# One kernel under an order of its own: a list scheduler, lanes in pairs, four shared PSUM tiles

## The chip, the cores and the metric

The kernel runs on one core of a Trainium2 chip. The metric is device time in microseconds (us). TensorE is called PE here, VectorE DVE, ScalarE ACT, GpSimd POOL and SyncE SP; PEld is PE's weight load.

## The reference, cut to what matters

All tensors are bf16, with S = 2048 positions, D = 640 channels and F = 1728. With x = q:

- `kv = shift(k) * v`, where shift is a causal convolution with 4 taps for each channel.
- `y = causal_conv(kv, ssm_k) + kv * ssm_D`: a convolution of length 2048 for each channel (an FFT of 4096 in the reference).
- `h = x + layernorm(x) * y`
- `out = h + (silu(z @ w_gate) * (z @ w_up)) @ w_down`, with `z = layernorm(h)`.

## The kernel before, in words

**Tiling.** The 2048 positions are cut into four blocks of 512 (`NB` = 4), and block i needs the blocks before it through the long convolution. The convolution is done in a transformed domain: `x_transform` (L289 to L317) multiplies kv by constant cosine and sine tables on PE (L300), evacuates on ACT (L133) and combines on DVE into six lanes, S, D and E for two parities. `g_load`, `g_fold` and `g_transform` (L218 to L268) do the same to the four pieces of the filter. `half_sum` (L213) makes each S lane of the filter.

**A block's convolution.** For block i the six accumulators are the sum over j of X[j] * H[i-j], lane by lane on DVE: products at L514, L522, L534 and L537, sums at L526 and L538. The lanes of filter pieces 1 to 3 and of blocks 0 and 1 go to DRAM on POOL's queue (`store_lane`, L206) and come back on SP's (`load_lane`, L210). `back` (L357 to L397) combines the accumulators on DVE, transforms them back on PE (L379), evacuates (L381), forms h, takes the layernorm's sums on ACT (`ln_stats`, L335 and L336; for block 0 partly on DVE, L332), the power on POOL (L346), and transposes the normalised h on PE (L395) into `hlnT`.

**A block's FFN.** `ffn` (L399 to L450): 27 passes of five gate or up matmuls (L428) into four one-bank PSUM tiles, Silu (L432) and copy (L433) on ACT, their product `tT` on DVE (L434); then 4 row tiles of 28 down matmuls (L444), evacuation (L447), the addition of h on DVE (L449), and the store on POOL's queue (L450).

**Order.** The tile framework's planner orders the instructions by priorities (`at`): block i's convolution has U*(i+1), its FFN U*(i+2.5), the rest of the filter (PREP) comes behind block 0's convolution. Every engine then carries out its own list in that order. PSUM is two two-bank tiles (`psM`) for all but gate and up, and four one-bank tiles (`psF`) for these. `hlnT` and `tT` have one buffer each, so the gate and up of block i+1 wait for the transposes of block i+1 and for the down matmuls of block i. At the start block 0's k is loaded in pieces (`load_k`, L154): the rows of partitions 16 to 127 on SP's queue, the rest in five small DMAs on ACT's queue, among ACT's own work.

Of the kernel before, what the change touches and what calls it, by code (L numbers as in the profile page):

```python
# [28 lines left out]
NSP, NWK, NWG = 20, 7, 3  # L29
LANES = [(l, e) for l in ("S", "D", "E") for e in range(2)]  # L30
# [6 lines left out]
def make_consts():  # L37

# [18 lines left out]
    po = -so[:, None] * np.sin(np.outer(to, m))  # L57
# [9 lines left out]
    return bf(cs), bf(gb), bf(ci)  # L67


@with_exitstack  # L70
def kernel(
# [45 lines left out]
    def spt(name):  # L117
        return sp.tile([P, 2, D], BF16, name=name, tag="sp", bufs=NSP)

    def h0t(name):  # L120
        return sp.tile([P, 2, D], BF16, name=name, bufs=1)

    def wkt(name, shape=(P, NS, D)):
        return wk.tile(list(shape), BF16, name=name, tag="wk", bufs=NWK)

    def ps_mm():
        return psM.tile([P, 2, 512], FP32, name="ps_mm")

    def evac(dst, ps, dve=False):
        if dve:  # L130
            nc.vector.tensor_copy(v2(dst), r3(ps))
        else:
            nc.scalar.copy(v2(dst), r3(ps))  # L133
# [19 lines left out]

    def load_k(i):  # L154
        kt = wk.tile([P, NS + 3, D], BF16, name="krun", bufs=1)
        if i == 0:
            nc.vector.memset(kt[0:1, 0:3, :], 0.0)
            nc.scalar.dma_start(out=kt[0:1, 3:7, :], in_=kk[0:NS, :].rearrange("(o r) d -> o r d", o=1))
            lo = P
            while lo > 1:  # L160

                hi, lo = lo, 16 if lo == P else lo // 2
                (nc.sync if hi == P else nc.scalar).dma_start(
                    out=flat(kt[lo:hi, :, :]),
                    in_=bass.AP(tensor=kk.tensor, offset=kk.offset + (NS * lo - 3) * D, ap=[[NS * D, hi - lo], [1, 7 * D]]))
        else:
            nc.sync.dma_start(out=flat(kt[:]), in_=rows(kk, i, -3, 7))
        return kt

    def load4(t, i, name):  # L170
        x = wkt(name)
        nc.sync.dma_start(out=flat(x[:]), in_=rows(t, i))
        return x

    cs_t = cpool.tile([P, NS, 2, HALF], BF16, name="cs_t")
    gb_t = cpool.tile([P, 2, 4, HALF], BF16, name="gb_t")
    ci_t = cpool.tile([P, 2, 2, NS, P], BF16, name="ci_t")
    wd_t = cpool.tile([P, 14, D], BF16, name="wd_t")
    w4 = cpool.tile([P, 4, D], BF16, name="w4")

    with at(1000):
        wrow = wk.tile([1, D, 4], BF16, name="wrow", tag="hlnT", bufs=1)
        nc.scalar.dma_start(out=wrow[:], in_=A_shift_k.rearrange("(o d) j -> o d j", o=1))
        D5 = cpool.tile([P, NDC, 1], BF16, name="D5")
        with nc.allow_non_contiguous_dma(reason="one column of 640 values"):
            nc.scalar.dma_start(out=D5[:], in_=A_ssm_D.rearrange("(c p o) -> p c o", p=P, o=1))
        ident = cpool.tile([P, P], BF16, name="ident")
        nc.scalar.dma_start(out=ident[:], in_=id_h.ap())
        ones1 = cpool.tile([1, P], BF16, name="ones1")
        nc.vector.memset(ones1[:], 1.0)  # L190
        twos1 = cpool.tile([1, P], BF16, name="twos1")
        nc.vector.memset(twos1[:], 2.0)
        mhalf = cpool.tile([P, NS], FP32, name="mhalf")
        nc.vector.memset(mhalf[:], -0.5)
        for j in range(4):
            pw = ps_mm()
            for h in range(2):
                nc.tensor.matmul(pw[:, h, 0:NH], ones1[:], wrow[:, h * NH:(h + 1) * NH, j], start=True, stop=True)
            nc.scalar.copy(v2(w4[:, j, :]), r3(pw))

    XD = [dram.tile([6, P, 2, D], BF16, name=f"xd{j}") for j in range(NB - 1)]
    HD = [None] + [dram.tile([6, P, 2, D], BF16, name=f"hd{p}") for p in range(1, NB)]
    lane_no = {le: n for n, le in enumerate(LANES)}

    def store_lane(dst, le, src):
        nc.gpsimd.dma_start(out=dst[lane_no[le]], in_=src[:])  # L206

    def load_lane(src, le):
        t = spt(f"ld{le[0]}{le[1]}")
        nc.sync.dma_start(out=t[:], in_=src[lane_no[le]])  # L210
        return t

    def half_sum(dst, a, b):  # L213
        nc.vector.tensor_add(dst[:], a[:], b[:])
        nc.vector.tensor_scalar_mul(dst[:], dst[:], 0.5)


    def g_load(p):  # L218
        gst = wk.tile([P, NDC, MBLK], BF16, name="gst", tag="h", bufs=2)
        nc.sync.dma_start(out=gst[:], in_=A_ssm_k[:, p * MBLK:(p + 1) * MBLK].rearrange("(c p) t -> p c t", p=P))  # L220
        return gst

    sprev = [None]

    def g_fold(p, gst):
        gf = wk.tile([P, 2, NDC, HALF], BF16, name="gf", tag="wgu", bufs=NWG)
        gu, gw = gf[:, 0], gf[:, 1]
        hi, lo = gst[:, :, HALF:MBLK], gst[:, :, HALF:0:-1]
        nc.vector.tensor_add(gu, hi, lo)
        nc.vector.tensor_sub(gw, hi, lo)  # L230
        if p == 0:
            sm = small.tile([P, NDC, 1], BF16, name="sm")
            nc.vector.tensor_add(sm[:], gst[:, :, 0:1], D5[:])
            nc.vector.tensor_scalar_mul(gw[:, :, 0:1], sm[:], 0.5)
        else:
            s = cpool.tile([P, NDC, 1], BF16, name=f"s{p}")
            if p == 1:
                nc.vector.tensor_copy(s[:], gst[:, :, 0:1])
            else:
# [12 lines left out]
    def g_transform(p, gT, dsts=None):
        lanes = {}
        for n, (nm, src) in enumerate((("Pe", 0), ("Me", 1), ("Po", 1), ("Mo", 0))):
            dst = dsts[n] if dsts else h0t(f"h0{nm}")[:] if p == 0 else spt(f"{nm}{p}")[:]
            delta = p == 0 and src == 0
            for c in range(2):
                ps = ps_mm()
                for h in range(2):
                    hs = slice(h * NH, (h + 1) * NH)  # L260
                    for tt in range(2):
                        nc.tensor.matmul(ps[:, h, 0:NH], gb_t[:, tt, n, c * P:(c + 1) * P], gT[:, src, tt, hs],  # L262
                                         start=(tt == 0), stop=(tt == 1 and not delta))
                    if delta:
                        nc.tensor.matmul(ps[:, h, 0:NH], twos1[:], gT[0:1, 1, 0, hs], start=False, stop=True)
                nc.scalar.copy(v2(dst[:, c, :]), r3(ps))
            lanes[nm] = dst
        return lanes  # L268


# [302 lines left out]
```

## Time and profile before

| what | value |
|---|---|
| median of 3 runs | 368.66 us (367.96 to 368.69) |
| profiled execution: time, span | 370.26 us, 368.5 us |
| PE busy | 276.9 us (75%) |
| DVE busy | 248.7 us (67%) |
| ACT busy | 190.8 us (52%) |
| POOL busy | 30.8 us (8%) |
| DMA | 62.44 MB, mean 169 GB/s |
| TensorE clock granted, mean | 0.904 of full speed |

The span runs from the first to the last instruction of the profiled execution; its time has 1.8 us more around it. Busy time is a mean over stages with different limits. Matmul times are modelled and overlap, so the length of a run of matmuls divided by their number tells more than the mean of one.

### The profile page before, as it was taken

To read this page: it belongs to the slowest core of one execution; us is meant where nothing else is said; L and a number is where in the kernel's file an instruction comes from. 1 tells how busy PE (TensorE), PEld (TensorE's weight loads), DVE (VectorE), ACT (ScalarE), POOL (GpSimd) and SP (SyncE) were. 2 spreads that over 40 slices of the span, in tenths; PEclk is the share of its full clock that TensorE was granted. 3 is DMA by queue.
4 is the path that set the end of the run, shared out by engine and by line. 5 is a ranking of instruction groups with operands and counts; after the bars stand their busy time and mean duration, and the time that the engine had idled before them with its cause. 6 is when DMAs were issued, how large, how long until landed. Compare 5 with 4: busy or idle time off the path is not lost.

```text
span 368.5 us, 4361 instructions
## 1 busy us (share of the span) xinstructions
PE 276.9 (75%) x1548; PEld 151.1 (41%) x1548; DVE 248.7 (67%) x408; ACT 190.8 (52%) x340; POOL 30.8 (8%) x50
## 2 busy tenths in 40 slices
PE   2490704386697997239999892999999579999992
PEld 0230402164453443126654451665445256544561
DVE  2129899697299999889679998997898320111100
ACT  4250300589984753744775484339755932355410
POOL 0000050100155200010100001001000010000000
PEclk9997585879999998858999997699999969999998
DMA  7990770023389999960509999922253500154000
GB/s 216 325 283 0 267 260 27 0 72 126 99 260 389 345 322 318 354 249 1 162 36 327 262 362 361 318 100 90 62 146 80 142 0 38 39 156 109 1 37 36
DMA packets 59321, 62.44 MB, mean 169 GB/s; under 512 B 13793, under 2 KB 48801, under 8 KB 58787
## 3 DMA queue, kind: packets, MB, share of 16 engines
q1 hardware_dynamic: 55424, 49.53, 43.6%
q0 software_dynamic: 3040, 12.45, 8.8%
q10 hardware_dynamic: 834, 0.18, 0.3%
q8 instruction: 12, 0.20, 0.2%
q14 instruction: 11, 0.09, 0.1%
HBM read 49.70 MB, written 12.45 MB: 169 GB/s over the span
## 4 chain that ended last, share of the span: by engine, by line
DVE 33%; PE 22%; issue 20%; ACT 11%; DMA 10%; POOL 2%; ACTq 0%; POOLq 0%; SPq 0%; DVEq 0%
PE ps_mm L444 9%; PE ps_mm L379 5%; DMA ident<-const_ident 3%; DVE tT L434 3%; PE ps_mm L300 3%; ACT gT L249 2%; DVE tp L534 2%; ACT junk L335 2%; DMA hd<-Mo 2%; ACT junk L336 2%; DMA ldD<-xd 2%; DMA krun<-in_A_k_dram 1%; PE ps_gu L428 1%; POOL rs L346 1%; PE ps_mm L262 1%
## 5 line engine op out<-in xcount | busy, mean ns | idle before, releaser
L428 PE MATMUL ps_gu<-hlnT,wgu 128*128 128x512 bf16 x540 | 120.0, 379 | 1.9 <-ACT sg L432 1.9
L428 PEld LDWEIGHTS <-wgu 128*128 128x128 bf16 x540 | 52.7, 98 | 63.6 <-issue 2.6
L444 PE MATMUL ps_mm<-wd_t,tT 128*128 128x320 bf16 x448 | 67.5, 308 | 0.2
L444 PEld LDWEIGHTS <-tT 128*128 128x128 bf16 x448 | 42.7, 100 | 24.9 <-issue 8.1
L432 ACT ACTIVATE sg<-ps_gu 128x512 bf16<-128x512 f32 (+1 forms) x56 | 33.5, 598 | 19.5 <-PE ps_gu L428 17.5
L433 ACT CAST uc<-ps_gu 128x512 bf16<-128x512 f32 (+1 forms) x56 | 32.9, 588 | 20.6 <-PE ps_gu L428 20.4
L434 DVE TENSOR_TENSOR tT<-sg,uc 128x512 bf16<-128x512 bf16 (+1 forms) x56 | 23.3, 418 | 27.5 <-ACT uc L433 27.5
L395 PE MATMUL ps_tr<-ident,hn 128*128 128x128 bf16 x80 | 11.2, 306 | 33.6 <-DVE hn L350 33.3
L447 ACT CAST o<-ps_mm 128x640 bf16<-128x640 f32 x16 | 11.0, 690 | 46.1 <-PE ps_mm L444 46.1
L300 PE MATMUL ps_mm<-kv,cs_t 128*128 128x320 bf16 x128 | 23.7, 329 | 12.2 <-DVE kv L286 11.4
L449 DVE TENSOR_TENSOR o<-o,h 128x1280 bf16<-128x1280 bf16 x8 | 6.6, 824 | 36.4 <-ACT o L447 36.3
L133 ACT CAST x<-ps_mm 128x640 bf16<-128x640 f32 x30 | 20.2, 710 | 18.5 <-PE ps_mm L300 17.7
L262 PE MATMUL ps_mm<-gT,gb_t 128*128 128x320 bf16 x128 | 24.9, 326 | 6.4 <-ACT gT L249 2.6
L381 ACT CAST y<-ps_mm 128x640 bf16<-128x640 f32 x16 | 11.1, 692 | 30.3 <-PE ps_mm L379 30.3
L379 PEld LDWEIGHTS <-ci_t 128*128 128x128 bf16 x128 | 13.8, 110 | 26.8 <-issue 13.8
L395 PEld LDWEIGHTS <-hn 128*128 128x128 bf16 x80 | 7.8, 137 | 37.6 <-DVE hn L350 36.0
L346 POOL TENSOR_TENSOR rs<-var,mhalf 128x4 f32<-128x4 f32 x8 | 9.6, 1205 | 160.2 <-DVE var L344 160.1
L300 PEld LDWEIGHTS <-cs_t 128*128 128x128 bf16 x128 | 13.4, 106 | 22.6 <-issue 15.3
L396 ACT COPY hlnT<-ps_tr 128x640 bf16<-128x640 bf16 x16 | 11.1, 692 | 16.4 <-PE ps_tr L395 16.0
L262 PEld LDWEIGHTS <-gb_t 128*128 128x128 bf16 x128 | 12.6, 103 | 16.8 <-issue 11.1
L285 DVE TENSOR_TENSOR kv<-kv,kt 128x2560 bf16<-128x2560 bf16 (+1 forms) x15 | 18.1, 1221 | 0.2
L281 DVE TENSOR_TENSOR kt<-krun,w 128x2560 bf16<-128x2560 bf16 (+1 forms) x15 | 18.1, 1221 | 0.1
(170 smaller groups left out, 360.7 us busy)
## 6 DMA issues: line engine op xcount, KB each, us to landing
wgu<-in_B_w_gate_dram SPq DMA_DIRECT2D x24, 320.0 KB, 3.4
wgu<-in_B_w_up_dram SPq DMA_DIRECT2D x24, 320.0 KB, 5.2
krun<-in_A_k_dram SPq DMA_DIRECT2D x3, 1120.0 KB, 5.3
ldS<-hd SPq DMA_DIRECT2D x10, 320.0 KB, 5.7
ldD<-hd SPq DMA_DIRECT2D x10, 320.0 KB, 5.4
ldE<-hd SPq DMA_DIRECT2D x10, 320.0 KB, 5.4
gst<-in_A_ssm_k_dram SPq DMA_DIRECT2D x4, 640.0 KB, 5.6
vt<-in_A_v_dram SPq DMA_DIRECT2D x4, 640.0 KB, 7.8
```

Of the source, the lines that this page charges most:

```text
L133: nc.scalar.copy(v2(dst), r3(ps))
L262: nc.tensor.matmul(ps[:, h, 0:NH], gb_t[:, tt, n, c * P:(c + 1) * P], gT[:, src, tt, hs], start=(tt == 0), stop=(tt == 1 and not delta))
L281: nc.vector.tensor_mul(dst[:, sl, :], ks, w4[:, j:j + 1, :].broadcast_to([P, n, D]))
L285: nc.vector.tensor_add(kv[:, sl, :], kv[:, sl, :], t[:, sl, :])
L300: nc.tensor.matmul(ps[:, h, 0:NH], cs_t[:, s, n, c * P:(c + 1) * P], kv[:, s, h * NH:(h + 1) * NH], start=(a == 0), stop=(a == 1))
L379: nc.tensor.matmul(ps[:, hh, 0:NH], ci_t[:, c, n, s, :], src[:, c, hh * NH:(hh + 1) * NH], start=(k == 0), stop=(k == 3))
L395: nc.tensor.transpose(pt[:, r, kt * P:(kt + 1) * P], hn[:, s, kt * P:(kt + 1) * P], ident[:])
L428: nc.tensor.matmul(ps[:], wgu[:, kt, off:off + P], hlnT[:, kt, :], start=(kt == 0), stop=(kt == NDC - 1))
L432: nc.scalar.activation(sg[0:np_, :], pss[0][0:np_, :], ACT.Silu)
L433: nc.scalar.copy(uc[0:np_, :], pss[-1][up_lo:up_lo + np_, :])
L434: nc.vector.tensor_mul(tT[0:np_, c, :], sg[0:np_, :], uc[0:np_, :])
L444: nc.tensor.matmul(ps[:, h, 0:NH], tT[0:np_, c, m * P:(m + 1) * P], wd_t[0:np_, c, h * NH:(h + 1) * NH], start=(c == 0), stop=(c == 13))
```

## The change: what it does

- **Order and buffers.** Each piece of work is recorded as an operation with engine, duration from a small table, reads, writes and buffers (`Plan.op`). `Plan.schedule` then simulates the engines: on each engine it takes the operation that can start first, at equal starts the one with the better priority. It hands out every buffer. The buffers of a class in SBUF are handed out in the order of the program. The operations are emitted in the order of their planned starts, under the framework's manual schedule, so each engine keeps that order. Some evacuations may go to ACT or DVE, whichever the plan finds free first.
- **PSUM.** Four two-bank tiles serve everything; gate and up of one pass share a tile.
- **Lanes in pairs.** S, D and E of one parity lie in one tile of 128 x 3840 (seven such tiles). A product or a sum over a block is one DVE operation of 3840 elements instead of three of 1280, and a load or store moves 960 KB instead of 320 KB. The signs and the order of the constant table `gb` are changed for this. In `back` the subtractions are two of 2560 instead of four of 1280.
- **Filter.** Piece 0 is folded on PE by an identity and a negative identity, after one reversing copy on ACT; the S lanes of piece 0 are made on PE (32 matmuls more and 8 of one row) instead of on DVE. The halving of the other S lanes may go to ACT or DVE. All filter pieces have a priority right behind block 0's own work.
- **Residual.** h is added in the down matmuls' accumulation by an identity, 2 matmuls for each row tile (32 in all); L449 is gone.
- **Layernorm.** All sums are on ACT (L332 is gone); h is treated in two halves of two row tiles, and each half has its own power on POOL.
- **Front.** Block 0's k comes in three DMAs: partitions 16 to 127 on SP's queue first of all, 1 to 15 and row 0 (in 16 pieces) on ACT's queue ahead of ACT's work; `ssm_D` comes on POOL's queue.

The core of the diff:

```diff
+OPT = ((0,), False, True, (0, 1, 2, 3))
...
-    po = -so[:, None] * np.sin(np.outer(to, m))
+    po = so[:, None] * np.sin(np.outer(to, m))
...
-    po[:, 0] = 2.0
+    po[:, 0] = -2.0
...
-        for n, b in enumerate((pe, me, po, mo)):
+        for n, b in enumerate((me, pe, mo, po)):
...
+
+    LAT = {"PE": 0.22, "DVE": 0.1, "ACT": 0.14, "POOL": 0.15, "SP": 0.1}
+    DMA_FIX, DMA_RATE = 1.6, 0.345e6
...
+            best = None
+            for e, lst in pend.items():
+                cand = None
...
+                    ok = True
+                    for b in o.allocs:
+                        if not b.cls.startswith("ps") and fifo[b.cls][0] is not b and not (len(o.allocs) > 1 and b in fifo[b.cls][:len(o.allocs)]):
+                            ok = False
+                            break
+                        if not free[b.cls]:
+                            ok = False
+                            break
+                        st = max(st, min(free[b.cls])[0])
+                    if not ok:
+                        continue
+                    key = (max(st, t0 + self.slack.get(e, 0)), o.pri, st, o.i)
+                    if cand is None or key < cand[0]:
+                        cand = (key, st, o, e)
+                if cand and (best is None or cand[1] < best[1]):
+                    best = cand
...
+            o.start = st
+            clock[o.eng] = st + o.dur
...
-    psM = ctx.enter_context(tc.tile_pool(name="psM", bufs=2, space=bass.MemoryType.PSUM))
-    psF = ctx.enter_context(tc.tile_pool(name="psF", bufs=4, space=bass.MemoryType.PSUM))
...
+    pl.klass("ps", [psum.tile([P, 2, 512], FP32, name=f"ps_{k}") for k in range(4)])
+    NLANE, NWK, NS25, NWG = 7, 6, 5, 3
+    klass("lane", NLANE, (P, 3, 2, D))
...
+    def c_tt(n, psum_in=False):
+        return 0.17 + 0.00104 * n if psum_in else 0.075 + 0.00052 * n
...
+    def c_act(n):
+        return 0.09 + 0.00078 * n
+
+    def c_mm(n):
+        return {512: 0.223, 320: 0.151, 128: 0.145}[n]
...
+            for k, (lo, hi, q) in enumerate(((16, P, "SP"), (1, 16, "ACT"))):
+                dma(lambda lo=lo, hi=hi: flat(kt.t[lo:hi, :, :]),
+                    lambda lo=lo, hi=hi: bass.AP(tensor=kk.tensor, offset=kk.offset + (NS * lo - 3) * D, ap=[[NS * D, hi - lo], [1, 7 * D]]),
+                    (hi - lo) * 7 * D * 2, w=[(kt, 4 << k)], q=q)
+            dma(lambda: flat(kt.t[0:1, 3:7, :]).rearrange("o (a b) -> o a b", a=16),
+                lambda: bass.AP(tensor=kk.tensor, offset=kk.offset, ap=[[NS * D, 1], [160, 16], [1, 160]]), 5 * KB, w=[(kt, 2)], q="ACT")
         else:
...
+        act(1.1, lambda: nc.scalar.copy(rv(), gview(gst)[:, :, HALF:0:-1]), [gst], [rev])
...
+                        nc.tensor.matmul(o, rv()[:, dc, tt * P:tt * P + P], (nident if n else ident).t[:], start=False, stop=True)
...
+    def g_transform_sum(gT):
...
+    def h_build(p, hp, hm):
+
+        for e in range(2):
...
+                  alt=[("DVE", c_ts(2 * D), lambda e=e: nc.vector.tensor_scalar_mul(hp[e].t[:, 2], hp[e].t[:, 2], 0.5))] if EITHER_G else [])
+            dma(lambda e=e: HDR[p, e].t[:], lambda e=e: hp[e].t[:], LANE_B, r=[hp[e]()], w=[HDR[p, e]], q="POOL")
...
+
+        for e in range(2):
+            def f(e=e):
+                a = acc[e].t
+                nc.vector.tensor_sub(a[:, 0:2], a[:, 2:3].broadcast_to([P, 2, 2, D]), a[:, 0:2])
+            dve(c_tt(4 * D), f, [acc[e]()], [acc[e](15)])
...
+            mvs.append(ln_stats(h, [r, r + 2], (), f"h{i}{r}"))
...
+                        oadd = part[0] == 0 and i in OADD_PE
+
+                        def mm(ps=ps, m=m, part=part, oadd=oadd):
+                            if oadd:
+                                for hh in range(2):
+                                    nc.tensor.matmul(ps.t[:, hh, 0:NH], ident.t[:], h.t[:, m, hh * NH:(hh + 1) * NH], start=True, stop=False)
...
+                    dve(c_tt(6 * D), lambda xl=xl, hl=hl: nc.vector.tensor_mul(xl.t[:], xl.t[:], hl.t[:]), [xl(), hl()], [xl()])
+                    if a is None:
+                        a = xl
+                    else:
+                        dve(c_tt(6 * D), lambda a=a, xl=xl: nc.vector.tensor_add(a.t[:], a.t[:], xl.t[:]), [a(), xl()], [a()])
...
+    order = pl.schedule()
+    with tc.manual_schedule():
+        for o in order:
+            o.fn()
```

## Rows read from the trace of the kernel before

**Rows 1.** Windows, whole span in six stretches; after the length, busy us (instructions).

```profile
core 0: us, PE busy (x) PEld busy (x) DVE busy (x) ACT busy (x) POOL busy (x), PEclk, DMA share, GB/s
0.00:28.50 28.50, 15.60 (x68) 6.97 (x68) 6.24 (x14) 11.74 (x15) 0.20 (x4) 1.00 0.86 266
28.50:60.30 31.80, 7.68 (x32) 4.23 (x33) 30.78 (x51) 4.15 (x6) 4.96 (x7) 0.65 0.43 161
60.30:77.60 17.30, 10.56 (x60) 6.79 (x61) 13.43 (x29) 8.75 (x16) 1.03 (x1) 0.70 0.00 0
77.60:106.80 29.20, 21.97 (x164) 14.25 (x163) 19.57 (x30) 28.14 (x47) 3.76 (x6) 0.97 0.44 139
106.80:297.00 190.20, 156.53 (x850) 82.83 (x848) 168.42 (x267) 113.17 (x217) 18.67 (x28) 0.92 0.69 220
297.00:368.50 71.50, 64.58 (x379) 36.02 (x379) 10.29 (x21) 24.84 (x40) 2.21 (x4) 0.95 0.19 54
```

**Rows 2.** Timeline of the front: start us, us, engine, line, tiles, [idle before].

```profile
4.91 0.83 DVE L229 TENSOR_TENSOR gf<-gst 128x1280 bf16<-128x1280 bf16 x1 [2.76 <-DMA gst<-in_A_ssm_k_dram]
...
6.05 0.29 ACTq L163 DMA_DIRECT2D krun<-in_A_k_dram  x1
...
20.97 4.59 PE L262 MATMUL ps_mm<-gT,gb_t 128*128 128x320 bf16 x18
...
23.33 0.23 ACTq L163 DMA_DIRECT2D krun<-in_A_k_dram  x1
...
28.51 0.82 DVE L281 TENSOR_TENSOR kv<-krun,w 128x1280 bf16<-128x1280 bf16 x1 [3.11 <-DMA krun<-in_A_k_dram]
```

**Rows 3.** Timeline of PE alone, around the transposes and the end.

```profile
162.96 2.90 PE L395 MATMUL ps_tr<-ident,hn 128*128 128x128 bf16 x20 [13.01 <-DVE hn L350]
...
232.80 17.75 PE L444 MATMUL ps_mm<-wd_t,tT 128*128 128x320 bf16 x112
...
300.02 16.59 PE L444 MATMUL ps_mm<-wd_t,tT 128*128 128x320 bf16 x112
316.54 29.31 PE L428 MATMUL ps_gu<-hlnT,wgu 128*128 128x512 bf16 x135
345.68 16.11 PE L444 MATMUL ps_mm<-wd_t,tT 128*128 128x320 bf16 x112
```

**Rows 4.** Groups by line, shapes apart: count | busy us, mean ns | idle.

```profile
L249 ACT COPY gT<-ps_tr 128x1280 bf16<-128x1280 bf16 x8 | 9.7, 1294 | 9.0 <-PE ps_tr L248 9.0
...
L335 ACT ACTIVATE junk<-h 128x640 bf16<-128x640 bf16 x14 | 10.5, 747 | 2.0 <-DVE h L385 1.7
...
L449 DVE TENSOR_TENSOR o<-o,h 128x1280 bf16<-128x1280 bf16 x8 | 6.6, 824 | 36.4 <-ACT o L447 36.3
...
L332 DVE BATCH_NORM_STATS2 bn<-xt 128x6 f32<-128x320 bf16 x8 | 3.4, 460 | 0.0
...
L335 ACT ACTIVATION_READ_ACCUMULATOR junk<-h 128x1 f32 x14 | 2.8, 199 | 0.0
...
L215 DVE TENSOR_SCALAR hS<-hS 128x1280 bf16<-128x1280 bf16 x4 | 1.8, 483 | 0.0
```

**Rows 5.** Timeline of DVE: two pairs of starts, one behind the other.

```profile
57.16 0.81 DVE L362 TENSOR_TENSOR accE<-accS,accE 128x1280 bf16<-128x1280 bf16 x1
57.90 0.81 DVE L362 TENSOR_TENSOR accD<-accS,accD 128x1280 bf16<-128x1280 bf16 x1
...
74.84 1.48 DVE L281 TENSOR_TENSOR kv<-krun,w 128x2560 bf16<-128x2560 bf16 x1
...
76.24 1.48 DVE L281 TENSOR_TENSOR kt<-krun,w 128x2560 bf16<-128x2560 bf16 x1
```

**Rows 6.** Windows, the stretch with the fullest DMA engines.

```profile
143.60:163.00 19.40, 6.28 (x33) 3.75 (x34) 16.90 (x30) 9.40 (x20) 1.47 (x1) 0.69 1.04 348
```

**Rows 7.** Timeline of the tail.

```profile
361.83 0.69 ACT L447 CAST o<-ps_mm 128x640 bf16<-128x640 f32 x1 [3.32 <-PE ps_mm L444]
...
363.67 0.54 POOL L450 DMA_DIRECT2D out_dram<-o  x1 [7.49 <-DVE o L449]
```

More of the change, by code (lines that the diff above doesn't have):

```diff
@@ new lines, with __init__, t, __call__ @@
+class Lane:
+    def __init__(self, b, e=None):
+        self.b, self.e = b, e
+    @property
+    def t(self):
+        if self.e is None:
+            return self.b.t
+        n = 6 * D
+        return self.b.t[:, self.e * n:(self.e + 1) * n].rearrange("p (l c d) -> p l c d", l=3, c=2)
+    def __call__(self, m=63):
+        return (self.b, m << (6 * (self.e or 0)))
+class Op:
+    __slots__ = ("i", "eng", "dur", "fn", "deps", "succ", "allocs", "frees", "pri", "nwait", "ready", "soft", "alts", "start", "end", "tag", "nbytes")
@@ L117, in spt @@
[L117 to L133, printed above, removed]
+    pool = ctx.enter_context(tc.tile_pool(name="sb", bufs=1))
@@ new lines, with sb, klass, __init__ @@
+    dram = ctx.enter_context(tc.tile_pool(name="dram", bufs=1, space=bass.MemoryType.DRAM))
+    psum = ctx.enter_context(tc.tile_pool(name="ps", bufs=1, space=bass.MemoryType.PSUM))
+    pl = Plan()
+    Plan.last = pl
+    pl.registry = []
+    pl.slack = {}
+    def sb(name, shape, dt=BF16):
+        return pool.tile(list(shape), dt, name=name)
+    def klass(name, n, shape, dt=BF16):
+        pl.klass(name, [sb(f"{name}_{k}", shape, dt) for k in range(n)])
+    class Fixed(Buf):
+        def __init__(self, name, shape, dt=BF16, where=None):
+            super().__init__(None, name)
+            self.slot = ((where or pool).tile(list(shape), dt, name=name), 0)
@@ new lines @@
+    twos1 = Fixed("twos1", (1, P))
+    mhalf = Fixed("mhalf", (P, NS), FP32)
+    junk = Fixed("junk", (P, D))
+    H0 = [Lane(Fixed(f"h0_{e}", (P, 3, 2, D))) for e in range(2)]
+    XDR = {(j, e): Fixed(f"xd{j}{e}", (P, 3, 2, D), where=dram) for j in range(2) for e in range(2)}
+    HDR = {(p, e): Fixed(f"hd{p}{e}", (P, 3, 2, D), where=dram) for p in range(1, NB) for e in range(2)}
+    LANE_B = P * 6 * D * 2
+    FOLD_PE, SUM_PE, EITHER_G, OADD_PE = OPT
+    CONV = [1000 * i for i in range(NB)]
@@ L178 @@
[L178 to L215, printed above, removed]
+    def load4(t, i, name, q="SP"):
+        x = B("wk", f"{name}{i}")
+        dma(lambda: flat(x.t[:]), lambda: rows(t, i), FULL, w=[x], q=q)
+        return x
@@ L256, in g_transform, with gTv @@
+    def gTv(gT):
+        return flat(gT.t[:]).rearrange("p (n a d) -> p n a d", n=2, a=2)
+    SRC = (1, 0, 0, 1)
+    def g_transform(p, gT, dst):
+        for b in (1, 0, 2, 3):
+            e, n = b // 2, b % 2
+            src = SRC[b]
             delta = p == 0 and src == 0
             for c in range(2):
[L258 to L265, printed above, removed]
@@ new lines, in mm @@
+                def mm(ps=ps, b=b, src=src, c=c, delta=delta):
+                    for h in range(2):
+                        hs = slice(h * NH, (h + 1) * NH)
+                        for tt in range(2):
+                            nc.tensor.matmul(ps.t[:, h, 0:NH], gb_t.t[:, tt, b, c * P:(c + 1) * P], gTv(gT)[:, src, tt, hs],
+                                             start=(tt == 0), stop=(tt == 1 and not delta))
+                        if delta:
+                            nc.tensor.matmul(ps.t[:, h, 0:NH], twos1.t[:], gTv(gT)[0:1, 1, 0, hs], start=False, stop=True)
@@ new lines, in shift, with tap @@
+    def shift(i, parts, kt, vt):
+        kv = B("wk", f"kv{i}")
+        tm = B("wk", f"tm{i}")
+        for sl in parts:
+            idx = range(*sl.indices(NS))
+            n, m = len(idx), sum(1 << s for s in idx)
+            def tap(dst, j, sl=sl, n=n):
+                ks = kt.t[:, 3 - j + sl.start:3 - j + sl.stop:sl.step, :]
+                nc.vector.tensor_mul(dst.t[:, sl, :], ks, w4.t[:, j:j + 1, :].broadcast_to([P, n, D]))
+            c = c_tt(n * D)
+            dve(c, lambda tap=tap: tap(kv, 0), [kt, (w4, 1)], [(kv, m)])
@@ new lines @@
+    pm = {0: H0}
+    h3 = B("wd", "h3")
+    with pl.at(CONV[0] + 50, "G"):
+        for p in range(1, NB):
+            gst = g_load(p)
+            gT = g_fold(p, gst)
+            pm[p] = [Lane(B("lane", f"H{p}{e}")) if p < 3 else Lane(h3, e) for e in range(2)]
+            g_transform(p, gT, pm[p])
+    with pl.at(CONV[0]):
+        state = back(0, acc, xt, mvx)
+        for e in range(2):
+            dma(lambda e=e, X=X: XDR[0, e].t[:], lambda e=e, X=X: X[e].t[:], LANE_B, r=[X[e]()], w=[XDR[0, e]], q="POOL")
```

809 lines of the change are left out of this document (520 added, 289 removed).

## The prediction

> **What bounds the kernel now.** I read the windows first, because a mean over the span hides the stages [rows 1]. They show three regimes. Up to 28.5 us DVE works 6.2 us and waits. From there to 297 us DVE is the busiest engine (30.8 of 31.8, 13.4 of 17.3, 19.6 of 29.2, 168.4 of 190.2), while PE works 156.5 of the 190.2. Behind 297 us PE alone works and DVE rests. The reader should add the DVE column up to 297: 238.4 us of work, 58.6 us idle, of which 22.3 in the front, 9.6 at 77.6 to 106.8 (ACT busy 28.1 of 29.2 there) and 21.8 in the long stretch.
>
> The timeline of the front says what the first idle time is: `krun`'s last pieces are issued on ACT's queue between ACT's own instructions, the first at 6.05 and the last at 23.33, and DVE's first tap starts at 28.51, let go by that DMA [rows 2]. The timeline of PE says why 71.5 us follow the convolutions: behind the last transposes come the down matmuls of block 2 (16.6 us), the gate and up of block 3 (29.3) and its down (16.1) [rows 3]. Block 2's down could have run earlier: PE stood 13.0 us before the transposes of block 1, let go by `hn` [rows 3], and some 7 us in each of the two later blocks, because its list had the transposes ahead of ready down matmuls.
>
> So the end is the time at which DVE has finished all four convolutions, plus what PE still owes then.
>
> **The change, part by part.** The sum is made against the profiled execution: span 368.5 us, time 370.26, which is 1.6 above the median of the three runs.
>
> *Front.* `krun` is now first on SP's queue and its rest first on ACT's. The front moved data at 266 GB/s [rows 1]; 1.12 MB take 4.2 us at that, and the first load of before, 640 KB issued at 0.74, let DVE go at 4.91 [rows 2]. I expect the first tap at about 8 us. Lower bound 7. Upper bound: if everything wanted early (k, v, the filter piece, two constant tables, 3.4 MB) shares the engines evenly, 3.4 MB / 266 GB/s = 13 and some 2 of latency, 15. Here a rule stands against the gain. The rows show the waits lie on ACT's queue (6.05 to 23.33) [rows 2], while the DMA engines of that stretch were 86% busy [rows 1]. The Trainium skill (DMA: Bandwidth & Descriptors, "Issuing engines are not separate DMA queues") says that DMAs from several queues interleave on the same 16 engines, so that another queue saves only the issuing. By that rule the front is bound by bytes and the tap starts at 15; by the rows on the queue it starts at 8.
>
> *DVE's work before the last `hn`.* Durations by distance of starts: 1280 elements 0.74 us, 2560 elements 1.40 [rows 5], so 0.66 for each further 1280 and 0.07 for an instruction.
> - Residual: 6 of the 8 L449 lie before that point, 6 x 0.74 = 4.4 [rows 4, 5].
> - L332: 8 on xt and 4 on h of the same shape, with their small partners, 12 x 0.46 = 5.5 [rows 4].
> - S lanes of piece 0: 2 x (0.74 + 0.41) = 2.3; fold of piece 0: 2 x 0.74 = 1.5 (a halving is 0.48 busy) [rows 4, 5].
> - Six more halvings that may go to ACT: half of them, 3 x 0.45 = 1.3.
> - Wide lanes: 90 products and sums become 30 of 3840; each saves two fixed parts, 30 x 0.14 = 4.2; the wider subtractions of `back` save 8 x 0.07 = 0.6. No row shows 3840 elements; below, nothing is saved.
> - Added: evacuations that the plan may hand to DVE at about 0.8 us each. There are 62 candidates; in the front ACT has more time free than DVE [rows 1], so I take 8 (6.4, less 1.6 for two that DVE has now): +5. Bounds 0 and 20 of them. The small statistics of h's second half: +1.5.
>
> Together -19.8 + 6.5 = -13.3: 225 us of work.
>
> *DVE's idle time before the last `hn`.* Front 8 until the first tap, and 5 more while the first transform runs. The 9.6 at 77.6 to 106.8 go: filter pieces 1 to 3 have priority behind block 0's own work, and ACT was idle 27.6 of 31.8 us in 28.5 to 60.3 [rows 1], which takes their evacuations. Of the 21.8 in the long stretch I keep 12, for DMA and PE; the last block's own latency (back transform, sums, power, `hn`) I put at 10, as its sums now go by halves. Sum 35. The last `hn` is at 225 + 35 = 260 instead of 297, and block 3's gate and up can start 3 us later, as they do now (297 to 300.02) [rows 3]: 263.
>
> *PE.* It must have done block 2's down by 263. In 106.8 to 297 it was busy 156.5 [rows 1]; with that down (16.6) and 24 identity matmuls at 16.11 / 112 = 0.144 (3.5) [rows 3] it is 177. Block 0's `hlnT` should be ready at about 64 (77.6 now, less 20 of the front, plus latency at a half-speed clock), so 199 us are open. It fits with 22 to spare, since any ready operation fills a gap. What the change adds on PE in the front, 32 matmuls of 0.26 at the lower clock (18 took 4.59) [rows 2], lies beside DVE's taps and costs nothing on the path; uncovered it would be 8.
>
> *End.* 263 + 29.3 + 16.1 + 8 x 0.144 = 309.6. The tail of before, from the end of the last matmul at 361.83 through ACT, DVE and the store issued at 363.67, is 6.7 us to 368.5 [rows 7]; without DVE's addition (0.85) 5.9. Span 315.5, with 1.8 around it and 1.6 down to the median: **315 us**.
>
> *Hidden at nothing:* ACT gets 6 more pairs of sums and up to 8 halvings of 1.29 [rows 4], some 20 us, in 131 us of idle time up to 297 [rows 1]; only block 0's two pairs on h lie on a path, 2 x 1.9 = 3.8 us if nothing covers them. Lane loads move the same bytes; the stretch with the fullest DMA engines (348 GB/s) cost DVE 2.5 of 19.4 us [rows 6], which is in the 12.
>
> **The rivals.**
> - *PE falls behind.* If the gaps are not filled in time, block 2's down still follows the last transposes: 315 + 16.6 = 332. For it: PE has only 22 us of slack. Against it: greedy filling.
> - *The plan does not hold on the chip,* that is, the change does not do what it says. The order is fixed, so one late instruction holds all behind it. For it: the table has 0.67 us for a sum on ACT and the rows 0.75 + 0.20, partly overlapped [rows 4]; it has 0.151 for a matmul that took 0.255 in the front [rows 2]. Then only the front (20.5) and some 5 of the work are won: 368.5 - 25 = 343.
> - *Bytes bound the front,* the first tap at 15: 322.
> - *Slower: PE at half clock.* With DVE the bound, PE pauses briefly between groups everywhere. Place: the 177 us of PE work from 64 to 263. Each us of it at 1.2 instead of 2.4 GHz costs one more; 22 are free, and the 53 us gained are gone when 75 of the 177 run at the low level; at 100 of them the time is 315 + 78 = 393. Rows: the granted clock was 0.65 and 0.70 where PE worked 24% and 61% of a stretch, 0.92 where it worked 82% [rows 1], which speaks against it. The Trainium skill (TensorE: Matmul & The Clock Gate, "A second HAM failure mode: psum-queue depth-cycling") says that short pauses from cycling through PSUM buffers can let the clock swing between its levels; four shared tiles cycle just so. By that rule the time is the 393 above; the trace's 0.92 with six tiles in use does not show it.
>
> **How the numbers follow.** Forecast, 300 to 326: 0.50. PE behind (332): 0.17. Plan not held (343): 0.17. Front by bytes (322): 0.06. Slower: 0.05. Below 300 (the low bounds together and more): 0.05. The range takes the bounds: 300 from the low ones (first tap at 7, no evacuations on DVE, mid idle 3), and 344 from the first tap at 15 (+7), twelve more evacuations (+8) and the idle time of before kept (+10), or from either of the two middle rivals. About 0.2% is what a measurement of this kernel can tell from no change. Faster by more: 0.94; within: 0.01; slower: 0.05.
>
> **What would show it.** Right: the first tap before 10 us; DVE's work before the last `hn` near 225 and idle time near 35; L395's last group near 262 with gate and up right behind it and no down matmuls between; the tail near 6 us. Wrong: down matmuls of block 2 behind the last transposes (first rival); DVE idle in many pieces let go by ACT or PE (second); a granted clock under 0.8 between 64 and 263 (the slower one). A first tap past 12 would fault the step on the front, more than 235 us of DVE work the step on the evacuations.

## The result: 327.9 us, where 315 was forecast

The changed kernel takes 327.91 us (median of 4 runs, 326.28 to 328.77), the kernel before 368.39 in the same session: ratio 0.890, 95% interval 0.886 to 0.893. The sign and the range (300 to 344) held, the size was 13 us short. The profiled execution has a span of 325.7 us where the sum gave 315.5. Two of the runs below were much slower than the others of their kernel (329.11 us of `e_three_taps`, 399.44 us of `e_best_wd_late` at a mean granted clock of 0.67) and are left out of the medians.

One correction first. The text ahead says that the S lanes of filter piece 0 are made on PE. The second entry of `OPT` is `False`, so `g_sum_dve` runs: two additions stay on DVE (L567), their halvings go to ACT (L568), and PE gets none of the 40 matmuls. I misread the option.

The windows of the kernel after, its span in seven stretches (after the length: busy us and, in brackets, instructions), as [rows 1] show them for before:

```profile
core 0: us, PE busy (x) PEld busy (x) DVE busy (x) ACT busy (x) POOL busy (x), PEclk, DMA share, GB/s
0.00:9.90 9.90, 2.42 (x8) 0.92 (x8) 2.83 (x6) 2.67 (x3) 1.20 (x5) 1.00 0.83 206
9.90:31.80 21.90, 16.15 (x106) 9.57 (x106) 20.92 (x31) 11.52 (x19) 0.56 (x1) 1.00 0.75 263
31.80:74.10 42.30, 31.81 (x221) 21.82 (x221) 36.73 (x62) 35.34 (x61) 2.97 (x4) 0.80 0.27 95
74.10:120.70 46.60, 36.27 (x166) 16.46 (x167) 45.29 (x52) 33.39 (x57) 4.34 (x8) 0.95 1.02 344
120.70:248.10 127.40, 116.67 (x671) 64.22 (x679) 120.22 (x148) 81.02 (x160) 15.34 (x11) 0.98 0.74 241
248.10:274.10 26.00, 24.42 (x173) 16.00 (x173) 8.06 (x20) 13.60 (x25) 1.99 (x3) 0.93 0.04 13
274.10:325.70 51.60, 46.33 (x253) 24.26 (x255) 5.95 (x14) 18.59 (x33) 1.63 (x3) 0.99 0.25 67
```

The front's wait is gone: DVE taps from 9.9 us. From 74 to 248 DVE is busy 165.5 of 174 us and PE 152.9, and up to 121 the DMA engines are full as well (share 1.02). From 248.1, DVE has little left to do (8.1 of 26.0 us, then 6.0 of 51.6) and PE works.

The timeline of PE, after, from block 2's gate and up to the end (start, us, engine, line, tiles, [idle before]):

```profile
227.79 16.73 PE L797 MATMUL ps<-hlnT,wgu 128*128 128x512 bf16 x74 [0.75 <-ACT uc L802]
248.10 3.38 PE L732 MATMUL ps<-wk,ci_t 128*128 128x320 bf16 x16 [3.58 <-ACT uc L802]
...
260.58 0.72 PE L751 MATMUL ps<-ident,s 128*128 128x128 bf16 x10
261.14 2.17 PE L822 MATMUL ps<-wd,tT 128*128 128x320 bf16 x14
264.88 0.81 PE L751 MATMUL ps<-ident,s 128*128 128x128 bf16 x10 [1.58 <-ACT s L827]
265.53 0.43 PE L818 MATMUL ps<-h,ident 128*128 128x320 bf16 x2
265.80 4.07 PE L822 MATMUL ps<-wd,tT 128*128 128x320 bf16 x28
269.80 0.45 PE L818 MATMUL ps<-h,ident 128*128 128x320 bf16 x2
270.08 4.07 PE L822 MATMUL ps<-wd,tT 128*128 128x320 bf16 x28
274.09 29.31 PE L797 MATMUL ps<-hlnT,wgu 128*128 128x512 bf16 x132
```

Compared with [rows 3], half of block 2's down (L822) now stands ahead of the last transposes (L751, 264.88) and half behind them: 8.6 us before block 3's gate and up can start, at 274.09. The forecast had them at 263. Each engine keeps the written order, so it was the plan that put them there: in its own times the last transposes start at 250.1 and block 3's gate and up at 260.7.

So the miss adds up on the span: last `hn` at 264.4 instead of 260 (+4.4), from it to gate and up 9.7 instead of 3 (+6.7), tail 5.0 instead of 5.9 (-0.9): 315.5 + 10.2 = 325.7.

### The profile page after: what moved, and what is told of

Its sections match the earlier page's. It is cut to its first block, busy times and chain, and to the rows that moved or that the text cites. A ratio compares the mean times of both kernels' runs of the same rounds, so it can differ in the third digit from the quotient of the medians.

```text
span 325.7 us, 4318 instructions
## 1 busy us (share of the span) xinstructions
PE 274.1 (84%) x1592; PEld 153.2 (47%) x1605; DVE 240.0 (74%) x329; ACT 196.1 (60%) x355; POOL 28.0 (9%) x35
## 4 chain that ended last, share of the span: by engine, by line
DVE 36%; issue 24%; PE 17%; ACT 16%; DMA 3%; POOL 2%; SPq 0%; POOLq 0%; DVEq 0%; ACTq 0%
PE ps L822 5%; DVE wk L616 5%; ACT junk L671 4%; DVE lane L928 4%; DMA h<-in_A_ssm_k_dram 3%; ACT junk L673 3%; PE ps L638 3%; DVE lane L927 3%; DVE tT L804 3%; PE ps L557 3%; PE ps L797 3%; DVE lane L706 3%; DVE wk L621 2%; DVE h L696 2%; DVE wk L714 1%
## 5 line engine op out<-in xcount | busy, mean ns | idle before, releaser
L797 PE MATMUL ps<-hlnT,wgu 128*128 128x512 bf16 x527 | 120.1, 383 | 6.0 <-ACT uc L802 3.3
L822 PE MATMUL ps<-wd,tT 128*128 128x320 bf16 x448 | 65.6, 299 | 0.0
L801 ACT ACTIVATE sg<-ps 128x512 bf16<-128x512 f32 (+1 forms) x56 | 33.3, 595 | 40.9 <-PE ps L797 37.2
L822 PEld LDWEIGHTS <-tT 128*128 128x128 bf16 x448 | 42.3, 98 | 19.8 <-issue 4.0
L802 ACT CAST uc<-ps 128x512 bf16<-128x512 f32 (+1 forms) x56 | 32.6, 582 | 4.3 <-DVE tT L804 3.2
L557 PE MATMUL ps<-wgu,gb_t 128*128 128x320 bf16 x128 | 25.1, 352 | 6.7 <-ACT wgu L351 4.0
L827 ACT CAST s<-ps 128x640 bf16<-128x640 f32 x16 | 11.0, 691 | 32.3 <-PE ps L822 32.3
L909 DVE TENSOR_TENSOR lane<-lane,lane 128x3840 bf16<-128x3840 bf16 x12 | 25.6, 2152 | 4.5 <-DMA lane<-xd 4.5
L616 DVE TENSOR_TENSOR wk<-krun,w 128x2560 bf16<-128x2560 bf16 (+1 forms) x20 | 24.1, 1221 | 4.7 <-DMA krun<-in_A_k_dram 4.5
L732 PEld LDWEIGHTS <-ci_t 128*128 128x128 bf16 x128 | 14.1, 112 | 18.5 <-DVE wk L714 10.3
L638 PE MATMUL ps<-wk,cs_t 128*128 128x320 bf16 x128 | 19.1, 302 | 4.3 <-ACT lane L351 2.4
L732 PE MATMUL ps<-wk,ci_t 128*128 128x320 bf16 x64 | 12.7, 363 | 9.9 <-DVE wk L714 6.3
L621 DVE TENSOR_TENSOR wk<-wk,wk 128x2560 bf16<-128x2560 bf16 (+1 forms) x15 | 18.3, 1221 | 0.2
L351 ACT CAST s<-ps 128x640 bf16<-128x640 f32 x16 | 11.1, 691 | 10.8 <-PE ps L732 10.7
L638 PEld LDWEIGHTS <-cs_t 128*128 128x128 bf16 x128 | 12.3, 99 | 10.9 <-issue 4.0
L671 ACT ACTIVATE junk<-h 128x640 bf16<-128x640 bf16 x16 | 11.8, 739 | 4.3 <-DVE h L738 4.0
```

Source lines behind the costliest of these rows:

```text
L351: nc.scalar.copy(dst(), src())
L557: nc.tensor.matmul(ps.t[:, h, 0:NH], gb_t.t[:, tt, b, c * P:(c + 1) * P], gTv(gT)[:, src, tt, hs], start=(tt == 0), stop=(tt == 1 and not ...
L616: nc.vector.tensor_mul(dst.t[:, sl, :], ks, w4.t[:, j:j + 1, :].broadcast_to([P, n, D]))
L638: nc.tensor.matmul(ps.t[:, h, 0:NH], cs_t.t[:, s, n, c * P:(c + 1) * P], kv.t[:, s, h * NH:(h + 1) * NH], start=(a == 0), stop=(a == 1))
L671: act(0.67, lambda s=s: nc.scalar.activation(junk.t[:], x.t[:, s, :], ACT.Identity, accum_out=st.t[:, s:s + 1]), [(x, 1 << s)], [(st, 1 << ...
L732: nc.tensor.matmul(ps.t[:, hh, 0:NH], ci_t.t[:, c, 1 - n, s, :], src[:, hh * NH:(hh + 1) * NH], start=(k == 0), stop=(k == 3))
```

## The experiments

Twelve kernels, each timed against the kernel before on its chip. The median of the kernel before was 366.68 to 368.77 us there, so a difference of 1 or 2 us between kernels of different sessions is read from the ratios (0.001 is 0.37 us). The code cuts are shortened. "Same written order" means that the plan is left as it is and only what an operation emits is changed, so that the rest of the order can't reshuffle.

**Is it PE, or DVE?** Four runs, same written order.

`e_no_res`, no residual:

```
-  if oadd: for hh in range(2): nc.tensor.matmul(ps.t[:, hh, 0:NH], ident.t[:], h.t[...], start=True, ...)
```

> Changed kernel, same written order, with the 32 identity matmuls that add the residual left out (the residual is missing from the output). Theory PE (from 74 us on the end is set by PE's own work): all 32 x 0.144 = 4.6 us come off, 323.3. Theory DVE (PE only follows the last hn): only those behind the last hn count, 8 of block 3 and 4 of block 2's two left-over row tiles, 12 x 0.144 = 1.7, 326.2.

Measured 328.50 us, ratio 0.891 (0.887 to 0.895): no gain. Theory PE is out, and theory DVE's 326.2 lies just below the interval (from 327.1 us on). In the profiled execution some of what was taken from PE came back in the last stretch, as the timeline of PE in this kernel shows:

```profile
247.83 4.43 PE L732 MATMUL ps<-wk,ci_t 128*128 128x320 bf16 x16 [3.57 <-ACT uc L802]
...
266.31 9.76 PE L819 MATMUL ps<-wd,tT 128*128 128x320 bf16 x56
276.00 29.31 PE L797 MATMUL ps<-hlnT,wgu 128*128 128x512 bf16 x135
```

Block 3's back transform starts 0.3 us earlier than in the changed kernel, but its 16 matmuls take 4.43 instead of 3.38 us and the 56 left-over down matmuls 9.76 instead of 8.1: over this stretch the mean granted clock was 0.85 instead of 0.93. PE lost there in speed what it had less to do. The three other runs have mean clocks of 0.945 to 0.950, close to the 0.946 to 0.958 of the changed kernel, and took 328.3 to 328.7 us all the same; no trace shows where the gain went in them.

`e_three_taps`, the fourth tap left out in all blocks:

```
-  for j in range(1, 4): tap(tm, j); kv += tm
+  for j in range(1, 3): tap(tm, j); kv += tm      (the plan still counts the fourth)
```

> Changed kernel, same written order, with the fourth tap of the short convolution left out (one product and one sum fewer in each part): DVE loses 3 x 2 x 1.40 + 4 x 0.86 = 11.8 us, PE nothing. Theory DVE: most of the 11.8 comes off, 316 to 318. Theory PE: only block 0's 3.4, which lets PE begin earlier, comes off, 324.5.

Measured 324.79, ratio 0.881 (0.874 to 0.888): some 3 us for 11.8 us of DVE's work (the interval still touches the changed kernel's). Theory DVE is out. The number is theory PE's 324.5, but not for its reason, the earlier start of block 0: `e_one_tap` below shows that block 0's taps alone give nothing. Block 3's back transform starts 5.3 us earlier (242.84), its gate and up 3.3 (270.83).

`e_thirds`, 3840 elements in three instructions:

```
-  nc.vector.tensor_mul(xl.t[:], xl.t[:], hl.t[:])
+  for l in range(3): nc.vector.tensor_mul(xl.t[:, l], xl.t[:, l], hl.t[:, l])      (so with all 30)
```

> Changed kernel, same written order, each of the 30 products and sums of 3840 elements written as three of 1280. DVE gets 30 x (3 x 0.74 - 2.07) = 4.5 us more, PE nothing. Theory DVE: 332.4. Theory PE: 328.0 to 328.5.

Measured 330.54, ratio 0.897 (0.892 to 0.901), between the two; the profiled span is 2.9 us longer. Wide lanes are worth some 2.6 us of the 4.5 that they take off DVE. Block 3's back transform starts 2.3 us later (250.40).

`e_both`, the first two together:

> Changed kernel, same written order, without the 32 identity matmuls and without the fourth tap (the residual is missing from the output). Alone they gave +0.6 and -2.5. If the order couples DVE and PE so that neither alone sets the end, together they give more than the sum: -7 or more, 321 or less. If DVE alone sets it: -2.5 again, 325. If a third thing does (ACT, the fixed waits): 325 too, with PE's and DVE's idle time both grown.

Measured 320.61, ratio 0.874 (0.868 to 0.880). By the medians that is -7.3, where the two alone gave +0.6 and -3.1, and I read it as coupling: in an order that cannot give way, work taken from one engine is waited for at the other. The numbers do not show that. The runs are of two sessions; by the ratios the pair gives -5.9 and the two alone +0.4 and -3.2, and the 3 us of difference lie within the intervals of the four ratios (together some 4 us). The traces also say where the difference arises. Block 3's back transform starts at 248.10 in the changed kernel, 247.83 without the residual, 242.84 without the fourth tap and 243.05 without both: up to there the two cuts add up to within 0.5 us. From there to block 3's gate and up the four take 26.0, 28.2, 28.0 and 25.3 us. The windows of that stretch in `e_no_res`, `e_three_taps` and `e_both`:

```profile
247.80:276.00 28.20, 26.14 (x164) 16.21 (x164) 8.10 (x20) 13.60 (x25) 1.99 (x3) 0.85 0.03 12
242.80:270.80 28.00, 26.05 (x172) 16.63 (x171) 8.11 (x20) 13.60 (x25) 1.99 (x3) 0.88 0.03 12
243.00:268.40 25.40, 23.37 (x165) 15.26 (x165) 8.11 (x20) 13.50 (x25) 1.99 (x3) 0.93 0.04 14
```

The two single cuts were profiled at a granted clock of 0.85 and 0.88 there, the pair and the changed kernel at 0.93. Why is not shown. What the runs do show is that DVE leads up to that point. PE's cut moves block 3's back transform by 0.3 of the 2.3 us that the 16 identity matmuls ahead of it take, and PE waits for DVE instead, already at block 1's back transform (timeline of PE, after and `e_no_res`):

```profile
120.73 4.45 PE L732 MATMUL ps<-wk,ci_t 128*128 128x320 bf16 x16 [5.92 <-DVE wk L714]
120.74 4.45 PE L732 MATMUL ps<-wk,ci_t 128*128 128x320 bf16 x16 [8.27 <-DVE wk L714]
```

Changes on DVE move it by about half: 5.3 of 11.8 us, and 2.3 of 4.5 in `e_thirds`. A cut that lies in block 0 alone gives less, 1.2 of 10.3 (`e_one_tap`, next).

**Does the start of block 0's FFN carry through?** I had put block 0's `hlnT` at 64; its gate and up start at 74.14.

`e_one_tap`, same written order, block 0's short convolution cut to one tap:

```
-  for j in range(1, 4): tap(tm, j); kv += tm
+  for j in range(1, 4 if i else 1): tap(tm, j); kv += tm      (the plan still counts them)
```

> Changed kernel, same written order, with block 0's short convolution cut to its first tap (six products and six sums of 0.86 us left out of DVE, 10.3 us, all of them before 24 us; blocks 1 to 3 as they were). Theory start (the end is the time at which block 0's gate and up start, 74.1, plus what DVE, PE and DMA share out from there): they start some 7 us earlier, since fewer taps in all blocks moved them by 2.4 for 3.4, and the end moves by as much, 320.5 to 321.5. Theory DVE work (any microsecond of DVE's counts alike): 10.3 x 2.5 / 11.8 = 2.2, 325.7. Rival (the front is bound by the filter block's load, its evacuations on ACT or the tables): start at 72 or later, 326 or more.

Measured 328.21, ratio 0.891 (0.887 to 0.896): nothing. My theory fell. The timeline of PE in this kernel shows the first reason:

```profile
12.87 0.29 PE L507 MATMUL ps<-ident,h 128*128 128x128 bf16 x1 [8.14 <-DMA h<-in_A_ssm_k_dram]
...
19.82 4.85 PE L638 MATMUL ps<-wk,cs_t 128*128 128x320 bf16 x32
```

In the written order the fold of filter piece 0 stands ahead of block 0's transform on PE, and it starts when the piece has landed, at 12.9 us. The transform cannot start before 19.8, however early the taps are done. Gate and up start 2.7 us earlier (71.45); block 1's back transform only 1.4 (119.29 instead of 120.73), since PE now waits 8.1 us for DVE there instead of 5.9; block 3's back transform 1.2 (246.89); its gate and up 0.2 (273.92), with a granted clock of 0.90 instead of 0.93 in between.

**Is the plan's table the fault?** The plan's own span is 313.3 us. Against the chip, its operations are 2 us late at the first tap, 3.4 at 23 us, 10 at 84, and then stay 9 to 15 late up to the end. The rows name terms that the table has too small:

```profile
L671 ACT ACTIVATE junk<-h 128x640 bf16<-128x640 bf16 x16 | 11.8, 739 | 4.3 <-DVE h L738 4.0
...
L671 ACT ACTIVATION_READ_ACCUMULATOR junk<-h 128x1 f32 x16 | 3.0, 189 | 0.0
```

(groups by line, after: count | busy us, mean ns | idle; on the timeline one sum starts 0.86 us behind the other, the table has 0.67) and, on the timeline of DVE, after:

```profile
12.37 0.83 DVE L616 TENSOR_TENSOR wk<-krun,w 128x1280 bf16<-128x1280 bf16 x1
13.23 0.82 DVE L621 TENSOR_TENSOR wk<-wk,wk 128x1280 bf16<-128x1280 bf16 x1
...
97.59 2.15 DVE L909 TENSOR_TENSOR lane<-lane,lane 128x3840 bf16<-128x3840 bf16 x1
99.66 0.42 DVE L804 TENSOR_TENSOR tT<-sg,uc 128x512 bf16<-128x512 bf16 x1
```

An operation that needs the one ahead of it starts 0.86 us behind it, where [rows 5] had 0.74 for independent ones; the taps of before alternated between the halves, those of after stand in a chain. A wide product takes 2.07.

`e_costs`, the table corrected:

```
-  lat = 0.0 if s.eng == o.eng ...                     act(0.67, ...) pow 1.2   DMA_FIX 1.6
+  lat = (0.12 if s.eng == "DVE" else 0.0) if ...      act(0.86, ...) pow 2.2 or 1.0   DMA_FIX 2.2
+  if e == "PE" and st < 74.0: o.dur *= 1.2
```

> Changed kernel with only the plan's table of costs corrected from its own trace: a sum on ACT 0.86 instead of 0.67 us, 0.12 between dependent operations of DVE instead of 0, PE operations started before 74 us 1.2 times as long, the power on POOL 2.2 or 1.0 instead of 1.2, a DMA's fixed time 2.2 instead of 1.6. The plan orders anew; its own span is 316.4 (313.3 with the old table). In the old order the corrected table adds up to 329. Theory costs (the 12 us between plan and chip are wrong costs held in a fixed order): 313 to 320. Theory bound (DVE's and PE's work itself sets the 326): within 2 of 327.9.

Measured 328.27, ratio 0.894 (0.889 to 0.900): no gain, the number of theory bound, although the operations now follow the plan within 3 us at the first taps and within 2 from there to 98 us. Then one wait breaks it, the first line of PE's waits (from 20 us on; us in total, times, longest), with the SP queue behind it:

```profile
PE ps L799 <- DMA wgu<-in_B_w_gate_dram: 8.2, 1, 8.2
```

```profile
86.37 11.86 SPq L372 DMA_DIRECT2D wd<-in_B_w_down_dram  x2
98.33 0.54 SPq L372 DMA_DIRECT2D wgu<-in_B_w_gate_dram  x1
98.97 1.14 SPq L372 DMA_DIRECT2D wgu<-in_B_w_up_dram  x1
100.16 5.84 SPq L372 DMA_DIRECT2D wk<-in_A_q_dram  x1
```

The down weights (2160 KB, first needed at 128) go out as soon as their buffer is free, their issue holds SP's queue for 11.9 us while the DMA engines are full, and the gate weights that PE wants next stand behind it. The plan has 0.46 us for an issue.

`e_wd_late` moves those two loads, in that order:

```
+  down = [o for o in order if o.eng == "SP" and o.nbytes in (13 * P * D * 2, 64 * D * 2)]
+  order = [o for o in order if o not in down]
+  k = max(i for i, o in enumerate(order) if o.eng == "SP" and o.tag == "F0") + 1
+  order[k:k] = down
```

> The kernel with the corrected table (328.3), and in its written order only the two loads of the down weights (2.16 MB) moved on SP's queue from before the last four groups of block 0's gate and up weights to behind them. There PE waited 8.2 us for a gate weight whose load stood behind the down weights. Theory queue order: that wait falls under 2 us and the time by 6, to 322. Rival theory bytes (the DMA engines were full from 80 to 128 us, so another load comes late instead, the down weights or the lanes): 326 to 329.

Measured 321.50, ratio 0.874 (0.869 to 0.878): -6.8 (-7.6 by the ratios), as the queue theory said: the same work in less time, so theory bound is out. PE's waits from 74 us on, and the window of the busiest part of the load, in this kernel:

```profile
PE ps L799 <- ACT uc L804: 7.3, 6, 3.3
PE ps L753 <- DVE s L698: 4.1, 4, 1.8
```

```profile
74.10:120.70 46.60, 39.76 (x193) 19.50 (x195) 42.97 (x55) 34.63 (x61) 5.95 (x9) 0.96 1.04 360
```

No wait for a gate weight is left among them; block 1's back transform starts at 114.32 instead of 121.85, block 3's gate and up at 267.22 instead of 273.96. The DMA engines are as full as before (share 1.04): it was the order of the loads and not their bytes that held PE. Some of the wait came back: PE's gate and up wait 7.3 us for ACT's copies instead of 4.5. Nor is a long issue a matter of the large load alone. In this kernel a gate weight of 320 KB, on its turn when the DMA engines are full, holds the queue for 6.9 us and the down weights behind it for 6.1:

```profile
90.63 6.89 SPq L372 DMA_DIRECT2D wgu<-in_B_w_gate_dram  x1
102.64 6.13 SPq L372 DMA_DIRECT2D wd<-in_B_w_down_dram  x2
```

`e_after_wd_late`, the same move with the old table:

> The same move in the changed kernel itself (327.9), where that wait was 2.0 us and block 1's back transform then waited 5.9 for DVE. DVE's lateness there decides, not the weights: 326.5 to 328. If DVE is late because the weights were (its products wait for gate and up): 323.

Measured 327.88, ratio 0.893 (0.889 to 0.897): nothing. In the old order that wait was 2.0 us, and block 1's back transform, which waited 5.9 for DVE, now waits 8.6 and still starts at 120.49 (120.73). The down weights hold the queue for 1.8 us only; a load of a lane behind them holds it for 10.8:

```profile
99.18 1.83 SPq L370 DMA_DIRECT2D wd<-in_B_w_down_dram  x2
104.79 10.75 SPq L370 DMA_DIRECT2D lane<-hd  x1
```

The table and the move give nothing alone and 6.4 us together (5.9 by the ratios), more than the intervals leave open.

`e_costs_best` (corrected table, `OPT` with no residual on PE, `FFN` at 1100 and `HB` at 55) and `e_best_wd_late` (the move besides):

> The corrected table, and besides the residual back on DVE for all blocks (PE 4.6 us less, DVE 8 x 0.74 more, 6 of them before the last hn) and other priorities for the filter blocks and for gate and up; its plan ends at 313.5. Theory costs: 3 us under the run with the table alone. Theory DVE (a microsecond of DVE's work before the last hn is a microsecond of the end): 4.4 us over it.

> The same move in the kernel that was at 322.2 and in which PE waited 8.4 us for the same gate weight. Queue order: 316. Bytes: 320 to 323.

Measured 322.22, ratio 0.878 (0.873 to 0.883), and 318.98, ratio 0.868 (0.864 to 0.871): the fastest here, 8.9 us under the changed kernel (8.2 by the ratios). The first came out 6.0 under `e_costs`, twice what its plan promised. The second gained 3.2 from the move (3.9 by the ratios), between the 316 of the queue theory and the 320 to 323 of its rival; its profile is of the run left out, so where the rest went is not shown. Residual and priorities were changed at once, so what each gives was not separated.

**Where do the 40 us come from?** `e_front`, the kernel before with only the early k:

```
+  with at(500): kt0 = load_k(0)            (ahead of all other loads)
-  hi, lo = lo, 16 if lo == P else lo // 2
+  hi, lo = lo, 16 if lo == P else 1        (three pieces instead of seven; D goes to POOL's queue)
```

> Kernel before, with only its front changed: the load of k for block 0 goes first on its queues and in three pieces instead of seven, and D is loaded on POOL's queue. If the front's wait passes through: the first tap at about 10 instead of 28.5 us, 368.4 - 18.5 = 350. Rival (the wait is taken up behind it by the filter piece, the tables or ACT's evacuations): 360 or more.

Measured 356.05, ratio 0.966 (0.962 to 0.971): -12.7 where the first tap came 16.5 us earlier (12.0 instead of 28.5). Most of it passes through, not all: the time lies between what the theory and its rival gave. The remaining 28 us of the change are its order and its operations together, and the 2 us by which its first tap is earlier still; apart from the wide lanes (`e_thirds`) no run here tells them from each other.

`e_prio`, the scheduler takes the highest priority and not the earliest start:

```
-  key = (max(st, t0 + self.slack.get(e, 0)), o.pri, st, o.i)
+  key = (o.pri, st, o.i)
```

> Changed kernel, one line of the scheduler changed: of the operations that could come next on an engine the one of the highest priority, whatever its start, instead of the one that can start first. Same operations and buffers. The plan's own span is 395.6. If filling the gaps is what the scheduler gives: 400 to 410. If the edits to the operations (wide lanes, early front, shared tiles) carry the gain: under 345.

Measured 415.75, ratio 1.130 (1.123 to 1.137), with the same operations. The first line of its waits on PE and on DVE (whole span):

```profile
PE ps L732 <- DVE wk L714: 53.8, 3, 17.9
```

```profile
DVE tT L804 <- ACT uc L802: 97.3, 45, 20.8
```

PE holds its queue for the transforms, and DVE waits for the evacuations of gate and up; that matmuls of the FFN were ready behind the transforms is argued from the order and not shown. So the rule of the earliest start is worth 88 us in this plan, and the theory that the edits to the operations carry the gain alone (under 345) is out. What the same operations would give under another order by priorities, such as that of the kernel before, is not shown.

## Why the prediction was right, and where it was short

*Front.* The first tap is at 9.91 us (8, with bounds 7 and 15). The rival of bytes is out for this step: `e_front` moves the same bytes in another order and brings the tap to 12.0. The Trainium skill (DMA: Bandwidth & Descriptors, "Issuing engines are not separate DMA queues") has the time to issue as the only saving from several queues, and calls it usually small. Here it was not small: the last piece of k was issued at 23.33 between ACT's own work, and in `e_front`, with k first and in three pieces, at 1.45. Behind the tap the bytes do tell: piece 0 lands at 12.9 and holds PE (`e_one_tap`).

*DVE before the last `hn`*: 234 us of work instead of 225 and 31 idle instead of 35, counted to the end of `hn` at 265.2 (it starts at 264.4, where 260 was forecast). The mis-sized term is the evacuations: 14 of 0.82 us lie on DVE (11.5), not 8 (6.4), so +5.1. The additions of the S lanes that I had moved to PE are +1.5; 7 of 8 halvings lie off DVE instead of 5, -0.9. Some 3 us are not accounted for; the chained taps are one candidate. The wide lanes save on DVE what I took, 30 x (3 x 0.74 - 2.07) = 4.5 for 4.2, but only 2.6 of it reach the end.

*PE.* This is the step that failed: "it fits with 22 to spare, since any ready operation fills a gap". The work was as forecast (177.35 us busy from 74.1 to 274.1), the start was not: 74.1, not 64, which took 10 of the 22. In what was left PE was idle 10.3 us up to 121, 5.9 of them for DVE, which was busy 45.3 of 46.6 us there beside full DMA engines, and 12.3 behind it. So the first rival, PE behind, came half true: 8.6 of the 16.6 us of block 2's down stand behind the last transposes, as they do in the plan. That an earlier start would have cured it was my explanation until `e_one_tap`. The runs show instead that up to block 3's back transform DVE leads and about half of a cut on it comes through (little of one in block 0), while a cut on PE is waited for at DVE; and that the order of the loads counts, 6.8 us, once the table is corrected. That PE and DVE hold one another is not shown, and what takes the other half of DVE's cuts stays open.

One reading ahead of the sum was wrong, without effect on it: the 0.26 us of a matmul in the front was put down to a lower clock, but the granted clock of that stretch is 1.00 [rows 1], and the 32 matmuls were never there. The terms of the range's upper end add up to 340, and twelve evacuations at 0.8 are 9.6, not 8; the 344 stands on the second rival (343).

*The plan does not hold* (343): on the changed kernel it was 12 us late, nearly all of it by 84 us. Correcting the table brought no gain by itself, so this was not the whole cause; with the two loads moved as well it did.

*Slower, PE at half clock:* out for the kernel as a whole, the granted clock is 0.95 from 74 to 121 and 0.98 from there to 248. The Trainium skill's rule that cycling through PSUM buffers makes the clock swing (TensorE: Matmul & The Clock Gate, "A second HAM failure mode: psum-queue depth-cycling") is not borne out by these rows with four shared tiles. A lower clock behind a single pause does show: 0.85 over 28 us in `e_no_res`, behind 3.6 us without work.

*Tail:* 5.0 us for 5.9; the rows are of ACT's evacuation and the last store's issue, as in [rows 7] without DVE's addition. From that issue to the end it is 4.0 us instead of 4.8:

```profile
320.71 0.69 ACT L827 CAST s<-ps 128x640 bf16<-128x640 f32 x1 [3.59 <-PE ps L822]
321.69 0.54 POOL L370 DMA_DIRECT2D out_dram<-s  x1 [8.03 <-ACT s L827]
```

*Open:* the 3 us of DVE's work, why only half of a change on DVE reaches block 3's back transform, and why the clock behind the pause there differs from kernel to kernel.

## What to carry to other kernels

In an order written ahead, ask of every load what stands behind it on its queue, and not only when its buffer is free: 2160 KB that nobody needed for another 40 us cost 6.8 in the kernel with the corrected table. When several engines are each some 90% busy, slack summed over a long stretch ("22 us to spare") is not slack; test with cuts on one engine and on two at once, and compare their traces stage by stage before you call a difference of a few microseconds coupling: here the excess lay in one stretch in which the clock differed. And correct a plan's costs from its own trace before judging its order, then look for the first wait that the table cannot hold.

## What the runs showed of the hardware

- While the DMA engines were full (shares of 1.02 and more), single issues held SP's queue for long, and not by size alone: the load of 2080 KB and its small partner for 10.6 us (after), 11.9 (`e_costs`), 6.1 (`e_wd_late`) and 1.8 (`e_after_wd_late`); one of 320 KB for 6.9 (`e_wd_late`); one of 960 KB for 10.8 (`e_after_wd_late`). Most issues of 320 KB from 74 to 110 us took 0.4 to 2.4.
- A dependent operation of 1280 elements on DVE starts 0.86 us behind the one that it needs, an independent one 0.74.
- After 3.6 us without work PE's next 16 matmuls took 3.38 us in one kernel and 4.43 in another: the mean granted clock of the 26 to 28 us from there on was 0.93 and 0.85. In `e_three_taps` and `e_both` it was 0.88 and 0.93, at the same place and behind the same pause.
